# A Fourier mixing layer and a leaky-ReLU feed-forward on one core: folding the sequence rows a second time

## The chip, the cores and the metric

The kernel runs on one core of one Trainium2 chip. The core has a matrix engine (TensorE, PE in the profile; its weight loads are a row of their own, PEld), a vector engine (DVE), a scalar engine (ACT), GpSimd (POOL) and SyncE (SP), which here issues DMAs. Each works through its own list of instructions in order, and waits on semaphores for the others. The metric is the device time of one execution in microseconds; the kernel before takes 2271.5 us (median of 3 runs, 2271.17 to 2273.4).

## What is computed

`x` is [8, 3008, 256] in fp32. Each batch goes through a two-dimensional Fourier transform, over the 3008 sequence rows and over the 256 features, of which the real part is kept. The result, taken as 24064 tokens of 256 features, goes through a feed-forward of width 2048:

```python
X = np.fft.fft(x, axis=1)
X = np.fft.fft(X, axis=2)
x = X.real.astype(np.float32).reshape(B * S, D)
h = x @ w_in                       # [24064, 2048]
g = np.maximum(0.01 * h, h)
out = (g @ w_out).astype(np.float32)
```

## The kernel before

All matmuls are fp32, and each stands in the trace as two matmul records. The feature transform is folded into `w_in` once: `w_in_part` multiplies the cosine and sine tables into it (`wf`, and `wn` for the one feature d = 128 that has no partner). The weights come as 64-bit words; `to_f32` turns one 128x512 piece into fp32 with seven DVE instructions (L218 to L224). There are eight such conversions for `w_in` and eight for `w_out`.

The sequence transform is a matmul with tables. The host lays `x` out so that a sequence row s stands beside its mirror S - s; `load_x` brings a batch into one x buffer as two DMAs of 1536 KB, and `fold_x` adds each row to its mirror (L170), then takes sums and differences of the features d and 256 - d (L172, L173). After that `z` has some 1505 rows that matter, the even and the odd ones apart, in NI = 6 tiles of 128 rows for each parity. A unit (b, c) is a batch and one half c of the frequencies k: 377 or 376 columns. `dft(u, blk)` makes for one unit and one of the two feature blocks (cosine, sine) two accumulated products, over even rows and over odd rows, of six matmuls each (L262). `butterfly` adds and subtracts the two and so gives both k and H + k (H = S/2). `nyquist(c)` does the same for the feature d = 128 of all eight batches, in 12 matmuls for each c.

Then come 32 blocks of 16 steps. A step (j, f) is `up`: two matmuls (L312) into two PSUM tiles, three DVE instructions (L314, L317, L318) that make the tile `g`, and a leaky ReLU on ACT (L319); and `down` (L329): four matmuls that accumulate `g` into four `sum` tiles. `down` trails `up` by `lag = 2` steps. The PSUM tag `up` has four buffers, which `up`, `dft`, `nyquist` and `w_in_part` share; `g` has five.

What stands around that is placed in the step loop at the end of `tile_fnet_leaky_relu`: two `dft` calls for the next unit in each odd block, `load_x(b + 1)` and `fold_x(b + 1)` once per batch. The order on each engine isn't the written one: a scheduler puts instructions forward when it holds their data ready, and the engine then keeps to that list. So the fold of the next batch stands between the DVE instructions of several steps. Before the loop stand the loads, the fold of batch 0, the eight conversions of `w_in`, the first unit's `dft`, and the eight conversions of `w_out`.

Of the kernel before, what the change touches and what calls it, by code (L numbers as in the profile page):

```python
# [28 lines left out]
F32 = mybir.dt.float32  # L32
I32 = mybir.dt.int32
U32 = mybir.dt.uint32
ALU = mybir.AluOpType
ACT = mybir.ActivationFunctionType

B, S, D, F = 8, 3008, 256, 2048
P = 128
H, Q = S // 2, S // 4  # L40
NI = 6
K0 = [0, 377]
KW = [377, 376]
KC = 377
NF = F // P
# [1 line left out]
SLOPE = 0.01  # L47


def m_order():  # L50

    m = np.full((P, NI), -1)
    for i in range(5):
        m[:, i] = 1 + P * i + np.arange(P)
    m[0:112, 5] = 641 + np.arange(112)
    m[112, 5] = 0
    return m


def laid_out(x):  # L60


    m = m_order()
    rows = np.where(m[:, :, None] < 0, S, 2 * m[:, :, None] + np.arange(2))
    mirrors = np.where(rows == S, S, (S - rows) % S)
    d = np.concatenate([np.arange(P + 1), np.arange(D - 1, P, -1)])
    x = np.concatenate([x, np.zeros((B, 1, D), x.dtype)], axis=1)
    return np.stack([x[:, rows][..., d], x[:, mirrors][..., (D - d) % D]], axis=1)


def seq_tables():

    m = m_order()
    out = np.zeros((4, 2, P, NI, KC), np.float32)
    for r in range(2):
        ok = (m >= 0) & ((m < Q) if r == 1 else True)
        weight = np.where(ok, 1.0, 0.0)
        if r == 0:
            weight = np.where((m == 0) | (m == Q), 0.5, weight)
        for c in range(2):  # L80
            k = K0[c] + np.arange(KW[c])
            turn = ((2 * m[:, :, None] + r) * k) % S
            turn = np.where(turn > H, turn - S, turn)
            a = 2.0 * np.pi * turn / S
            cos = np.where(4 * np.abs(turn) == S, 0.0, np.cos(a))
            sin = np.where(np.abs(turn) == H, 0.0, np.sin(a))
            out[r, c, :, :, : KW[c]] = weight[:, :, None] * cos
            out[2 + r, c, :, :, : KW[c]] = weight[:, :, None] * sin
    return out
# [28 lines left out]
def columns():

    at = np.zeros(B * S, np.int64)  # L120
    for b, c, sg, first, n in chunks()[0]:
        k = K0[c] + np.arange(n)
        plus, minus = (k, (S - k) % S) if sg == 0 else ((H + k) % S, H - k)
        at[b * S + minus] = first + n + np.arange(n)
        at[b * S + plus] = first + np.arange(n)
    return at
# [3 lines left out]
def tile_fnet_leaky_relu(  # L130
# [10 lines left out]
    nc = tc.nc  # L141
    PS = bass.MemoryType.PSUM
    const = ctx.enter_context(tc.tile_pool(name="const", bufs=1))
    xp = ctx.enter_context(tc.tile_pool(name="xp", bufs=1))
# [7 lines left out]
    def dft_ps():  # L152
        return up_ps("dft_ps")
# [1 line left out]
    xs = {}  # L155

    def load_x(b):
        t = xp.tile([P, 2, NI, 2, D], F32, tag="x", bufs=1, name="xt")
        for h in range(2):
            nc.sync.dma_start(t[:, h], x[b, h])  # L160
        xs[b] = t

    zs = {}

    def fold_x(b):

        t = xs.pop(b)
        s = t[:, 0].rearrange("p i r d -> p (i r) d")
        z = t[:, 1].rearrange("p i r d -> p (i r) d")
        nc.vector.tensor_tensor(s, s, z, op=ALU.add)  # L170
        lo, hi = s[:, :, 1:P], s[:, :, P + 1 : D]
        nc.vector.tensor_tensor(z[:, :, 1:P], lo, hi, op=ALU.add)  # L172
        nc.vector.tensor_tensor(z[:, :, P + 1 : D], lo, hi, op=ALU.subtract)  # L173
        nc.scalar.copy(z[:, :, 0:1], s[:, :, 0:1])
        nc.gpsimd.memset(z[:, :, P : P + 1], 0.0)
        zs[b] = z


    feat_sb = const.tile([P, 2, 2 * P + 2], F32, name="feat_sb")
    nc.sync.dma_start(feat_sb, feat_tab.rearrange("(a p) n -> p a n", p=P))  # L180
    load_x(0)
    wf = const.tile([P, 2, F], F32, name="wf")
    wn = const.tile([P, NF], F32, name="wn")
    wo = const.tile([P, NF, D], F32, name="wo")
    nyx = const.tile([P, 2, NI, 2, B], F32, name="nyx")
    nya = nyx[:, 0]
    tabs = {}

    def load_tab(q, n, c):
        t = const.tile([P, NI, KC], F32, name=f"tab_{n}_{c}")  # L190
        q.dma_start(t, seq_tab[n, c])
        tabs[n, c] = t
# [54 lines left out]
    def w_out_part(f):  # L247
        nf = WN // D
        raw = load_w(w_out[f * P : (f + nf) * P, :].rearrange("(c p) d -> p c d", p=P))
        to_f32(wo[:, f : f + nf, :].rearrange("p c d -> p (c d)"), raw, w_out.dtype)  # L250

    fold_x(0)
    for n in range(4):
        load_tab(nc.scalar, n, 0)
# [4 lines left out]
    def sequence(ps_t, m, z_of, n, c):  # L259

        for i in range(NI):
            nc.tensor.matmul(ps_t[0:m, 0 : KW[c]], lhsT=z_of(i), rhs=tabs[n, c][:, i, 0 : KW[c]],  # L262
                             start=(i == 0), stop=(i == NI - 1))

    def butterfly(plus, minus, even_ps, odd_ps, m, kw):
        ev = work.tile([P, KC], F32, tag="ev", bufs=2, name="ev")
        nc.scalar.copy(ev[0:m, 0:kw], even_ps[0:m, 0:kw])  # L267
        nc.vector.tensor_tensor(plus, ev[0:m, 0:kw], odd_ps[0:m, 0:kw], op=ALU.add)  # L268
        nc.vector.tensor_tensor(minus, ev[0:m, 0:kw], odd_ps[0:m, 0:kw], op=ALU.subtract)  # L269

    def dft(u, blk):

        b, c = u
        z, kw = zs[b], KW[c]
        t = work.tile([P, 2, KC], F32, tag=f"mix{blk}", bufs=2, name=f"mix{blk}")
        pe, po = dft_ps(), dft_ps()
        for r, pt in ((0, pe), (1, po)):
            sequence(pt, P, lambda i: z[:, 2 * i + r, blk * P : (blk + 1) * P], 2 * blk + r, c)
        butterfly(t[:, 0, 0:kw], t[:, 1, 0:kw], pe, po, P, kw)
        mixed.setdefault(u, {})[blk] = t  # L280


    nc.vector.tensor_tensor(nya, nya, nyx[:, 1], op=ALU.add)
    nyq_dram = dram.tile([B, 2, 2, KC], F32, name="nyq_dram")

    def nyquist(c):
        pe, po = dft_ps(), dft_ps()
        for r, pt in ((0, pe), (1, po)):
            sequence(pt, B, lambda i: nya[:, i, r, :], r, c)
        t = work.tile([P, 2, KC], F32, tag="mix0", bufs=2, name="nyq")  # L290
        butterfly(t[0:B, 0, 0 : KW[c]], t[0:B, 1, 0 : KW[c]], pe, po, B, KW[c])
        nc.sync.dma_start(nyq_dram[:, c, :, 0 : KW[c]], t[0:B, :, 0 : KW[c]])
# [29 lines left out]
    def down(j, f):  # L322
# [8 lines left out]
        if f == NF - 1:  # L331
            for h in range(2):
                o = work.tile([P, 2, KC], F32, tag="o", bufs=2, name="o")
                for i in range(2):
                    nc.scalar.copy(o[:, i, 0:n], sums[j][h][i][:, 0:n])  # L335
                nc.sync.dma_start(out[h * P : (h + 1) * P, first : first + 2 * n].rearrange("p (i n) -> p i n", i=2),
                                  o[:, :, 0:n])

    nyquist(0)
    dft(units[0], 0)  # L340
    dft(units[0], 1)
    spread(units[0])
# [53 lines left out]
```

## Time and profile before

| what | value |
|---|---|
| median of 3 runs | 2271.5 us |
| the profiled execution's own time | 2273.85 us |
| its span, first to last instruction | 2272.1 us |
| PE busy | 2229.8 us, 98% |
| DVE busy | 963.7 us, 42% |
| ACT busy | 502.7 us, 22% |
| DMA, mean rate | 33 GB/s |
| mean granted TensorE clock | 0.998 of full speed |

The busy times are averages over two quite different stretches: a start of some 65 us, in which loads and conversions run, and the loop. The profiled execution lies 1.75 us over its span, and 2.35 us over the median.

### The profile page before, as it was taken

The page shows a single profiled execution, that of the slowest core. Times are in us where ns is not written, and L with a number is a line of the kernel's source. Part 1 is how long each engine was busy: PE and PEld are TensorE (multiplying, and loading weights), DVE is VectorE, ACT ScalarE, POOL GpSimd, SP SyncE. Part 2 cuts the span into 40 slices and gives each one's busy share as a digit, 9 for nine tenths or more (in the row PEclk, how much of TensorE's full clock was granted, in tenths as well). Part 3 has the DMA queues.
Part 4 walks back from the last instruction along what each step waited for, and adds up shares of the span by engine and source line. Part 5 has one row for each costly group of instructions (what it writes and reads, how often), then busy time and mean ns, then how long its engine had stood idle before and what let it go on. Part 6 is the DMA issues. An engine that isn't in the chain of part 4 may idle for free.

```text
span 2272.1 us, 18025 instructions
## 1 busy us (share of the span) xinstructions
PE 2229.8 (98%) x7056; PEld 1329.0 (58%) x7056; DVE 963.7 (42%) x1741; ACT 502.7 (22%) x696; POOL 1.2 (0%) x12
## 2 busy tenths in 40 slices
PE   3999999999999999999999999999999999999999
PEld 1555655555555565555555556555655555555565
DVE  5734434344343433435334353334434344343343
ACT  0122222222122221222222122221222222222222
POOL 0000000000000000000000000000000000000000
PEclk9999999999999999999999999999999999999999
DMA  7201000010000200001000100001000010000000
GB/s 299 89 14 61 16 14 21 14 74 2 14 21 14 76 14 1 21 29 62 14 8 14 70 21 14 21 14 56 21 14 21 14 62 14 14 21 14 14 14 14
DMA packets 23965, 75.23 MB, mean 33 GB/s; under 512 B 1968, under 2 KB 12608, under 8 KB 20808
## 3 DMA queue, kind: packets, MB, share of 16 engines
q1 hardware_dynamic: 22728, 64.82, 7.7%
q10 hardware_dynamic: 1152, 9.27, 1.0%
q8 instruction: 55, 0.90, 0.2%
q14 instruction: 30, 0.25, 0.0%
HBM read 49.35 MB, written 24.72 MB: 33 GB/s over the span
## 4 chain that ended last, share of the span: by engine, by line
PE 98%; DMA 1%; DVE 1%; SPq 0%; issue 0%; ACT 0%; DVEq 0%
PE sum_ps L329 57%; PE cos_ps L312 14%; PE sin_ps L312 14%; PE dft_ps L262 11%; DMA raw<-in_w_in_dram 1%; PE up_ps L238 0%; PE up_ps L243 0%; DVE win L224 0%; DVE raw L223 0%; DVE raw L219 0%; DVE raw L222 0%; DVE xt L172 0%; DVE xt L173 0%; DVE raw L218 0%; DVE raw L221 0%; DVE raw L220 0%
## 5 line engine op out<-in xcount | busy, mean ns | idle before, releaser
L329 PE MATMUL sum_ps<-g,wo 128*128 128x377 f32 (+1 forms) x4096 | 1379.4, 479 | 0.0
L329 PEld LDWEIGHTS sum_ps<-g,wo 128*128 128x128 f32 x4096 | 777.1, 190 | 519.4 <-ACT g L319 0.2
L319 ACT ACTIVATE g<-g 128x752 f32<-128x752 f32 (+1 forms) x512 | 426.0, 832 | 1516.6 <-DVE g L318 1513.6
L314 DVE SCALAR_TENSOR_TENSOR cos<-nb,wn,cos_ps 128x376 f32<-128x376 f32 (+1 forms) x512 | 310.5, 607 | 1007.9 <-PE cos_ps L312 1007.9
L312 PE MATMUL sin_ps<-mix,wf 128*128 128x376 f32 (+1 forms) x1024 | 407.4, 479 | 0.0
L312 PE MATMUL cos_ps<-mix,wf 128*128 128x376 f32 (+1 forms) x1024 | 406.7, 478 | 0.0
L317 DVE TENSOR_TENSOR g<-cos,sin_ps 128x376 f32<-128x376 f32 (+1 forms) x512 | 280.3, 547 | 62.9 <-DVE cos L314 1.9
L318 DVE TENSOR_TENSOR g<-cos,sin_ps 128x376 f32<-128x376 f32 (+1 forms) x512 | 276.8, 541 | 0.0
L312 PEld LDWEIGHTS sin_ps<-mix,wf 128*128 128x128 f32 x1024 | 194.1, 190 | 129.9
L312 PEld LDWEIGHTS cos_ps<-mix,wf 128*128 128x128 f32 x1024 | 193.0, 189 | 130.9 <-issue 0.6
L262 PE MATMUL dft_ps<-tab,xt 128*128 128x377 f32 (+1 forms) x768 | 248.4, 479 | 0.0
L262 PEld LDWEIGHTS dft_ps<-tab,xt 128*128 128x128 f32 x768 | 145.3, 189 | 98.2 <-issue 0.6
L268 DVE TENSOR_TENSOR mix<-ev,dft_ps 128x377 f32<-128x377 f32 (+1 forms) x32 | 17.5, 547 | 196.3 <-PE dft_ps L262 189.8
L335 ACT COPY o<-sum_ps 128x376 f32<-128x376 f32 (+1 forms) x128 | 53.9, 474 | 77.5 <-PE sum_ps L329 77.5
L238 PE MATMUL up_ps<-win,feat_sb 128*128 128x512 f32 x32 | 19.9, 758 | 38.2 <-DVE win L224 38.2
L170 DVE TENSOR_TENSOR xt<-xt 128x3072 f32<-128x3072 f32 x8 | 26.8, 3352 | 22.3 <-DMA xt<-in_x_dram 22.3
L238 PEld LDWEIGHTS up_ps<-win,feat_sb 128*128 128x128 f32 x32 | 6.4, 222 | 45.4 <-DVE win L224 39.1
L267 ACT COPY ev<-dft_ps 128x377 f32<-128x377 f32 (+3 forms) x34 | 16.1, 473 | 75.7 <-PE dft_ps L262 75.7
L269 DVE TENSOR_TENSOR mix<-ev,dft_ps 128x377 f32<-128x377 f32 (+1 forms) x32 | 17.3, 541 | 0.0
L262 PE MATMUL dft_ps<-tab,nyx 128*8 128x377 f32 (+1 forms) x48 | 15.7, 479 | 0.0
L172 DVE TENSOR_TENSOR xt<-xt 128x1524 f32<-128x1524 f32 x8 | 13.9, 1738 | 0.0
L173 DVE TENSOR_TENSOR xt<-xt 128x1524 f32<-128x1524 f32 x8 | 13.9, 1737 | 0.0
(24 smaller groups left out, 94.7 us busy)
## 6 DMA issues: line engine op xcount, KB each, us to landing
xt<-in_x_dram SPq DMA_DIRECT2D x16, 1536.0 KB, 9.5
out_dram<-o SPq DMA_DIRECT2D x32, 377.0 KB, 2.6
out_dram<-o SPq DMA_DIRECT2D x32, 376.0 KB, 2.8
tab<-in_seq_tab_dram ACTq DMA_DIRECT2D x8, 1131.0 KB, 10.0
raw<-in_w_in_dram SPq DMA_DIRECT2D x8, 512.0 KB, 3.9
raw<-in_w_out_dram SPq DMA_DIRECT2D x8, 512.0 KB, 3.7
nb<-nyq_dram SPq DMA_DIRECT2D x8, 377.0 KB, 3.3
nb<-nyq_dram SPq DMA_DIRECT2D x8, 376.0 KB, 4.0
```

The source lines that it names most:

```text
L170: nc.vector.tensor_tensor(s, s, z, op=ALU.add)
L238: nc.tensor.matmul(pt, lhsT=feat_sb[:, a, w * P : (w + 1) * P], rhs=win[a], start=(a == 0), stop=(a == 1))
L262: nc.tensor.matmul(ps_t[0:m, 0 : KW[c]], lhsT=z_of(i), rhs=tabs[n, c][:, i, 0 : KW[c]], start=(i == 0), stop=(i == NI - 1))
L268: nc.vector.tensor_tensor(plus, ev[0:m, 0:kw], odd_ps[0:m, 0:kw], op=ALU.add)
L269: nc.vector.tensor_tensor(minus, ev[0:m, 0:kw], odd_ps[0:m, 0:kw], op=ALU.subtract)
L312: nc.tensor.matmul(pt[blk][:, 0:n], lhsT=wf[:, blk, fs], rhs=mixed[b, c][blk][:, sg, 0:n], start=True, stop=True)
L314: nc.vector.scalar_tensor_tensor(cos[:, 0:n], in0=spreads[b, c][:, sg, 0:n], scalar=wn[:, f : f + 1], in1=pt[0][:, 0:n], op0=ALU.mult, op1 ...
L317: nc.vector.tensor_tensor(g[:, 0, 0:n], cos[:, 0:n], pt[1][:, 0:n], op=ALU.add)
L318: nc.vector.tensor_tensor(g[:, 1, 0:n], cos[:, 0:n], pt[1][:, 0:n], op=ALU.subtract)
L319: nc.scalar.activation(g[:, :, 0:n], g[:, :, 0:n], ACT.Lrelu)
L329: nc.tensor.matmul(sums[j][h][i][:, 0:n], lhsT=wo[:, f, h * P : (h + 1) * P], rhs=g[:, i, 0:n], start=(f == 0), stop=(f == NF - 1))
L335: nc.scalar.copy(o[:, i, 0:n], sums[j][h][i][:, 0:n])
```

## The change

The fold is done twice. The host now lays four rows together, s, S - s, H - s and H + s, for s up to S/4, and `fold_x` first adds the mirrors (one instruction over both halves of the buffer), then takes the feature sums and differences for each half, and then adds and subtracts the two halves. The sum serves the even k, the difference the odd k (for the sine block the other way round, `(c + blk) % 2`). So a unit's c now means the parity of k and no longer the lower or upper half; the column counts stay 377 and 376. Each product over rows has NI = 3 tiles where it had 6, and each table half the bytes. `nyquist` gets the same second fold in two more small instructions. The x buffers become two.

```diff
-NI = 6
-K0 = [0, 377]
+NI = 3
...
-            k = K0[c] + np.arange(KW[c])
-            turn = ((2 * m[:, :, None] + r) * k) % S
+            k = 2 * np.arange(KW[c]) + c
+            turn = (s[:, :, None] * k) % S
...
     def load_x(b):
-        t = xp.tile([P, 2, NI, 2, D], F32, tag="x", bufs=1, name="xt")
+        t = xp.tile([P, 2, 2, NI * 2, D], F32, tag="x", bufs=2, name="xt")
         for h in range(2):
-            nc.sync.dma_start(t[:, h], x[b, h])
+            nc.sync.dma_start(t[:, h], x[b, :, h].rearrange("p e i r d -> p e (i r) d"))
         xs[b] = t
...
     def fold_x(b):
 
+
         t = xs.pop(b)
-        s = t[:, 0].rearrange("p i r d -> p (i r) d")
-        z = t[:, 1].rearrange("p i r d -> p (i r) d")
-        nc.vector.tensor_tensor(s, s, z, op=ALU.add)
-        lo, hi = s[:, :, 1:P], s[:, :, P + 1 : D]
-        nc.vector.tensor_tensor(z[:, :, 1:P], lo, hi, op=ALU.add)
-        nc.vector.tensor_tensor(z[:, :, P + 1 : D], lo, hi, op=ALU.subtract)
-        nc.scalar.copy(z[:, :, 0:1], s[:, :, 0:1])
-        nc.gpsimd.memset(z[:, :, P : P + 1], 0.0)
-        zs[b] = z
+        a, z = t[:, :, 0], t[:, :, 1]
+        nc.vector.tensor_tensor(a, a, z, op=ALU.add)
+        for h in range(2):
+            lo, hi = a[:, h, :, 1:P], a[:, h, :, P + 1 : D]
+            nc.vector.tensor_tensor(z[:, h, :, 1:P], lo, hi, op=ALU.add)
+            nc.vector.tensor_tensor(z[:, h, :, P + 1 : D], lo, hi, op=ALU.subtract)
+            nc.scalar.copy(z[:, h, :, 0:1], a[:, h, :, 0:1])
+            nc.gpsimd.memset(z[:, h, :, P : P + 1], 0.0)
+        nc.vector.tensor_tensor(a[:, 0], z[:, 0], z[:, 1], op=ALU.add)
+        nc.vector.tensor_tensor(a[:, 1], z[:, 0], z[:, 1], op=ALU.subtract)
+        zs[b] = a
...
-            sequence(pt, P, lambda i: z[:, 2 * i + r, blk * P : (blk + 1) * P], 2 * blk + r, c)
+            sequence(pt, P, lambda i: z[:, (c + blk) % 2, 2 * i + r, blk * P : (blk + 1) * P], 2 * blk + r, c)
...
-    nc.vector.tensor_tensor(nya, nya, nyx[:, 1], op=ALU.add)
+    nya, nyb = nyx[:, :, 0], nyx[:, :, 1]
+    nc.vector.tensor_tensor(nyb, nya, nyb, op=ALU.add)
+    nc.vector.tensor_tensor(nya[:, 0], nyb[:, 0], nyb[:, 1], op=ALU.add)
+    nc.vector.tensor_tensor(nya[:, 1], nyb[:, 0], nyb[:, 1], op=ALU.subtract)
```

The change also moves instructions, since the second x buffer lets a load and its fold go forward. In the lists below the changed kernel's lines are 3 to 8 higher than before's: its L223 to L229 are the seven instructions of a conversion, L173 is the first instruction of the fold, L176 and L177 are the feature sums and differences, L180 and L181 the second fold, L322, L325 and L326 the three of `up`.

DVE at the start, the second conversion of `w_in`, before:

```order
L218 TENSOR_SCALAR raw_105<-raw_102 128x512
L220 TENSOR_SCALAR raw_105<-raw_102 128x512
L219 SCALAR_TENSOR_TENSOR raw_105<-raw_102,raw_105 128x512
L221 TENSOR_SCALAR raw_105<-raw_105 128x512
L222 TENSOR_SCALAR raw_105<-raw_105 128x512
L223 SCALAR_TENSOR_TENSOR raw_105<-raw_102,raw_105 128x512
L224 SCALAR_TENSOR_TENSOR win_104<-raw_105 128x512
```

And the same conversion now, where `xt_816` is the second x buffer, batch 1:

```order
L223 TENSOR_SCALAR raw_111<-raw_108 128x512
L225 TENSOR_SCALAR raw_111<-raw_108 128x512
L224 SCALAR_TENSOR_TENSOR raw_111<-raw_108,raw_111 128x512
L226 TENSOR_SCALAR raw_111<-raw_111 128x512
L173 TENSOR_TENSOR xt_816<-xt_816 128x2x1536
L227 TENSOR_SCALAR raw_111<-raw_111 128x512
L176 TENSOR_TENSOR xt_816<-xt_816 128x6x127
L228 SCALAR_TENSOR_TENSOR raw_111<-raw_108,raw_111 128x512
L177 TENSOR_TENSOR xt_816<-xt_816 128x6x127
L229 SCALAR_TENSOR_TENSOR win_110<-raw_111 128x512
```

The fold of batch 1 has moved from the loop into conversions 2 to 4 of `w_in` (its other four instructions stand in conversions 3 and 4). On SP the two loads of batch 1 have moved with it, in front of the second and the third load of `w_in`.

DVE at the end of the start, the last conversion of `w_out` and the first step, before:

```order
L223 SCALAR_TENSOR_TENSOR raw_394<-raw_392,raw_394 128x512
L224 SCALAR_TENSOR_TENSOR wo_76<-raw_394 128x512
L268 TENSOR_TENSOR nyq_416<-ev_417,dft_ps_403 8x376
L269 TENSOR_TENSOR nyq_416<-ev_417,dft_ps_403 8x376
L314 SCALAR_TENSOR_TENSOR cos_426<-nb_312,wn_75,cos_ps_422 128x377
L317 TENSOR_TENSOR g_428<-cos_426,sin_ps_423 128x377
L318 TENSOR_TENSOR g_428<-cos_426,sin_ps_423 128x377
```

And now, from the last row but one of the fifth conversion of `w_out` on:

```order
L325 TENSOR_TENSOR g_412<-cos_410,sin_ps_407 128x377
L229 SCALAR_TENSOR_TENSOR wo_76<-raw_354 128x512
L223 TENSOR_SCALAR raw_364<-raw_362 128x512
L225 TENSOR_SCALAR raw_364<-raw_362 128x512
L224 SCALAR_TENSOR_TENSOR raw_364<-raw_362,raw_364 128x512
L226 TENSOR_SCALAR raw_364<-raw_364 128x512
L326 TENSOR_TENSOR g_412<-cos_410,sin_ps_407 128x377
L227 TENSOR_SCALAR raw_364<-raw_364 128x512
L322 SCALAR_TENSOR_TENSOR cos_420<-nb_302,wn_75,cos_ps_416 128x377
L228 SCALAR_TENSOR_TENSOR raw_364<-raw_362,raw_364 128x512
L325 TENSOR_TENSOR g_422<-cos_420,sin_ps_417 128x377
```

Before, the first step came behind all eight conversions; now the first four steps stand between the instructions of the last four conversions.

DVE in the loop, where a fold stands between steps (before it is batch 1, `xt_844`):

```order
L314 SCALAR_TENSOR_TENSOR cos_855<-nb_312,wn_75,cos_ps_851 128x377
L170 TENSOR_TENSOR xt_844<-xt_844 128x3072
L317 TENSOR_TENSOR g_857<-cos_855,sin_ps_852 128x377
L318 TENSOR_TENSOR g_857<-cos_855,sin_ps_852 128x377
L314 SCALAR_TENSOR_TENSOR cos_869<-nb_312,wn_75,cos_ps_865 128x377
L172 TENSOR_TENSOR xt_844<-xt_844 128x12x127
L317 TENSOR_TENSOR g_871<-cos_869,sin_ps_866 128x377
```

And now, at the same step of the same block (it is batch 2, `xt_1830`):

```order
L322 SCALAR_TENSOR_TENSOR cos_827<-nb_302,wn_75,cos_ps_823 128x377
L173 TENSOR_TENSOR xt_1830<-xt_1830 128x2x1536
L325 TENSOR_TENSOR g_829<-cos_827,sin_ps_824 128x377
L326 TENSOR_TENSOR g_829<-cos_827,sin_ps_824 128x377
L322 SCALAR_TENSOR_TENSOR cos_841<-nb_302,wn_75,cos_ps_837 128x377
L176 TENSOR_TENSOR xt_1830<-xt_1830 128x6x127
L325 TENSOR_TENSOR g_843<-cos_841,sin_ps_838 128x377
L326 TENSOR_TENSOR g_843<-cos_841,sin_ps_838 128x377
L177 TENSOR_TENSOR xt_1830<-xt_1830 128x6x127
L322 SCALAR_TENSOR_TENSOR cos_855<-nb_302,wn_75,cos_ps_851 128x377
```

The fold begins at the same place, three steps behind the `dft` that frees its buffer, a batch further ahead, and goes over four steps: one with L173, two with two feature instructions each, one with L180 and L181.

## Rows read from the trace of the kernel before

**Rows 1.** The page, busy time, share and instructions of each engine.
```profile
PE 2229.8 (98%) x7056; PEld 1329.0 (58%) x7056; DVE 963.7 (42%) x1741; ACT 502.7 (22%) x696; POOL 1.2 (0%) x12
```
**Rows 2.** By stretch: length, busy PE, PEld, DVE, ACT, POOL; clock, DMA share, GB/s.
```profile
100.00:2260.00 2160.00, 2160.00 (x6828) 1293.29 (x6827) 893.30 (x1610) 489.13 (x671) 0.84 (x7) 1.00 0.07 24
```
**Rows 3.** The chain that ended last: start us, us, what.
```profile
66.79 28.92 PE dft_ps L262 x90
...
160.57 7.59 PE dft_ps L262 x24
...
297.24 7.62 PE dft_ps L262 x24
...
2104.88 7.59 PE dft_ps L262 x24
```
**Rows 4.** Timeline of DVE, 22 to 34 us: start us, us, what, idle before.
```profile
22.33 3.36 DVE L170 TENSOR_TENSOR xt<-xt 128x3072 f32<-128x3072 f32 x1 [22.33 <-DMA xt<-in_x_dram]
...
26.64 1.74 DVE L172 TENSOR_TENSOR xt<-xt 128x1524 f32<-128x1524 f32 x1
28.30 1.74 DVE L173 TENSOR_TENSOR xt<-xt 128x1524 f32<-128x1524 f32 x1
...
30.89 0.25 DVE L283 TENSOR_TENSOR nyx<-nyx 128x96 f32<-128x96 f32 x1
```
**Rows 5.** DVE by stretch: length, busy, clock, DMA share, GB/s.
```profile
22.33:96.72 74.39, 65.94 (x124) 0.95 0.50 177
```
**Rows 6.** Timeline of DVE, 58 to 99 us: a wait in a conversion, first steps.
```profile
58.51 0.69 DVE L224 SCALAR_TENSOR_TENSOR win<-raw 128x512 f32<-128x512 f32 x1 [2.39 <-PE up_ps L243]
...
96.72 0.59 DVE L314 SCALAR_TENSOR_TENSOR cos<-nb,wn,cos_ps 128x377 f32<-128x377 f32 x1
...
98.34 0.60 DVE L314 SCALAR_TENSOR_TENSOR cos<-nb,wn,cos_ps 128x377 f32<-128x377 f32 x1
```
**Rows 7.** The chain: the `down` matmuls of the fourth step.
```profile
111.12 2.54 PE sum_ps L329 x8
```
**Rows 8.** Busy time by stretch, 2 to 22 us and 42 to 60 us.
```profile
2.00:22.00 20.00, 0.00 (x0) 0.00 (x0) 0.00 (x0) 0.00 (x0) 0.00 (x0) 1.00 0.98 407
42.00:50.00 8.00, 5.85 (x25) 3.63 (x26) 7.34 (x16) 1.33 (x3) 0.00 (x0) 1.00 0.39 131
50.00:53.00 3.00, 2.46 (x6) 1.05 (x4) 2.83 (x6) 0.00 (x0) 0.00 (x0) 0.61 0.53 175
53.00:57.00 4.00, 3.88 (x7) 1.82 (x7) 2.88 (x7) 0.65 (x2) 0.00 (x0) 0.50 0.42 131
```
**Rows 9.** Timeline of PE, 45 to 57 us.
```profile
45.47 1.98 PE L238 MATMUL up_ps<-win,feat_sb 128*128 128x512 f32 x4 [1.50 <-DVE win L224]
...
53.12 3.78 PE L238 MATMUL up_ps<-win,feat_sb 128*128 128x512 f32 x4 [0.66 <-DVE win L224]
```
**Rows 10.** The page, DMA issues: KB each, median us to landing.
```profile
xt<-in_x_dram SPq DMA_DIRECT2D x16, 1536.0 KB, 9.5
...
tab<-in_seq_tab_dram ACTq DMA_DIRECT2D x8, 1131.0 KB, 10.0
```
**Rows 11.** Timeline of DVE, 201 to 221 us, around a fold in the loop.
```profile
202.96 0.54 DVE L318 TENSOR_TENSOR g<-cos,sin_ps 128x377 f32<-128x377 f32 x1
205.58 0.61 DVE L314 SCALAR_TENSOR_TENSOR cos<-nb,wn,cos_ps 128x377 f32<-128x377 f32 x1 [2.08 <-PE cos_ps L312]
...
209.91 3.35 DVE L170 TENSOR_TENSOR xt<-xt 128x3072 f32<-128x3072 f32 x1
...
220.80 0.61 DVE L314 SCALAR_TENSOR_TENSOR cos<-nb,wn,cos_ps 128x377 f32<-128x377 f32 x1 [0.45 <-PE cos_ps L312]
```
**Rows 12.** Timeline of PE, the second `up` after that step's.
```profile
208.55 0.80 PE L312 MATMUL cos_ps<-mix,wf 128*128 128x377 f32 x2
```
**Rows 13.** Timeline of SP: the loads of batch 1 go out.
```profile
198.64 0.82 SPq L160 DMA_DIRECT2D xt<-in_x_dram  x2
```
**Rows 14.** The load line's instructions, time from issue to landing.
```profile
DMA to landing us min/median/max: 6.1/9.5/20.5
```

More of the change, by code (lines that the diff above doesn't have):

```diff
@@ L47, with m_order, taken @@
 SLOPE = 0.01
[L50 to L57, printed above, removed]
+def m_order(r):
+    m = np.arange(P)[:, None] + P * np.arange(NI)
+    return np.where(m < (377, 376)[r], m, -1)
 def laid_out(x):
-    m = m_order()
-    rows = np.where(m[:, :, None] < 0, S, 2 * m[:, :, None] + np.arange(2))
-    mirrors = np.where(rows == S, S, (S - rows) % S)
+    m = np.stack([m_order(0), m_order(1)], axis=-1)
+    rows = 2 * m + np.arange(2)
     d = np.concatenate([np.arange(P + 1), np.arange(D - 1, P, -1)])
     x = np.concatenate([x, np.zeros((B, 1, D), x.dtype)], axis=1)
-    return np.stack([x[:, rows][..., d], x[:, mirrors][..., (D - d) % D]], axis=1)
+    def taken(rows, d):
+        return x[:, np.where(m < 0, S, rows % S)][..., d]
+    mirrored = (D - d) % D
+    return np.stack([
+        np.stack([taken(rows, d), taken(S - rows, mirrored)], axis=2),
+        np.stack([taken(H - rows, d), taken(H + rows, mirrored)], axis=2),
+    ], axis=2)
 def seq_tables():
-    m = m_order()
     out = np.zeros((4, 2, P, NI, KC), np.float32)
     for r in range(2):
[L76 to L79, printed above, removed]
+        m = m_order(r)
+        s = 2 * m + r
+        weight = np.where(m < 0, 0.0, np.where((s == 0) | (s == Q), 0.5, 1.0))
         for c in range(2):
-            k = K0[c] + np.arange(KW[c])
-            turn = ((2 * m[:, :, None] + r) * k) % S
+            k = 2 * np.arange(KW[c]) + c
+            turn = (s[:, :, None] * k) % S
             turn = np.where(turn > H, turn - S, turn)
@@ L121, in columns @@
     for b, c, sg, first, n in chunks()[0]:
-        k = K0[c] + np.arange(n)
+        k = 2 * np.arange(n) + c
         plus, minus = (k, (S - k) % S) if sg == 0 else ((H + k) % S, H - k)
@@ L184, in tile_fnet_leaky_relu @@
     wo = const.tile([P, NF, D], F32, name="wo")
-    nyx = const.tile([P, 2, NI, 2, B], F32, name="nyx")
-    nya = nyx[:, 0]
+    nyx = const.tile([P, 2, 2, NI, 2, B], F32, name="nyx")
     tabs = {}
@@ L288, in nyquist @@
         for r, pt in ((0, pe), (1, po)):
-            sequence(pt, B, lambda i: nya[:, i, r, :], r, c)
+            sequence(pt, B, lambda i: nya[:, c, i, r, :], r, c)
         t = work.tile([P, 2, KC], F32, tag="mix0", bufs=2, name="nyq")
@@ L374 @@
         "x": x,
-        "x_nyq": x[..., P].transpose(2, 1, 3, 4, 0),
+        "x_nyq": x[..., P].transpose(1, 2, 3, 4, 5, 0),
         "w_in": moe_w_in,
```

## The prediction

> **What bounds the kernel now.** I read the busy times first: PE is busy for 2229.8 of 2272.1 us, DVE for 963.7 [rows 1]. A share over the whole span hides stages, so I looked by stretch: between 100 and 2260 us PE is busy for 2160.00 of 2160.00 us, at the full clock [rows 2]. Nothing else can be the bound there, and a matmul taken out shortens the time by its own length, as long as no other engine falls behind. The reader is to see that "busy" is the right number in this case: the chain of waits runs through PE's records without a gap, and gives the lengths end to end. A piece of 24 records of the sequence transform takes 7.59 us with 376 columns and 7.62 us with 377 [rows 3], so 0.316 us a record, two records to a matmul.
>
> The start is another kernel. DVE waits until x lands at 22.33 us [rows 4], DMA being the bound until then (407 GB/s, engines 98% busy [rows 8]). From there to 96.72 us, where the first step begins, DVE is busy for 65.94 of 74.39 us [rows 5], while PE takes its parts of `w_in` whenever a conversion is done, and from 66.79 us on has 28.92 us of transforms [rows 3]. So DVE and PE end the start nearly together: at 95.71 us PE is through, at 96.72 DVE.
>
> **PE in the loop.** Units 1 to 15 have two `dft` pieces each, 30 pieces of 24 records, of which the first, one with 377 columns and the last are shown [rows 3]; 16 belong to units with 376 columns and 14 to units with 377. Each piece keeps 12 records. What goes is 16 x 3.795 + 14 x 3.81 = 60.7 + 53.3 = 114.1 us. The `up` and `down` matmuls stay as they are, and so do the column counts. PE waits for nothing there, so all of it should come off the span, if DVE keeps pace.
>
> **DVE in the loop.** The old fold has 3072, 1524 and 1524 elements: 3.36 us and twice 1.74, of which a follower hides 0.08 (L172 and L173 start 1.66 apart) [rows 4]. The lengths give (3.36 - 1.74) / 1548 = 1.05 ns an element. By that an instruction of 762 elements takes some 0.87 us start to start and one of 1536 some 1.67. The new fold is 3.28 + 4 x 0.87 + 2 x 1.67 = 10.1 us where the old one was 6.6. It is off PE's path if DVE's delay stays below what the loop allows. A step is 12 records on PE, 3.8 us, in which DVE idles 2.08 [rows 11]. The three instructions of the step that ends at 202.96 + 0.54 = 203.5 us free the PSUM tiles that the second next `up` takes at 208.55 [rows 11, 12]: 5.05 us to spare. The worst delay now is after L173: 3.28 - 2.08 = 1.2 us; two steps with 1.74 us each take 0.7 back, the step with the two halves of 3.34 brings 1.3, so at most some 1.8. The old fold did the same, 3.35 us in one step [rows 11], and DVE was back at waiting for PE by 220.80 us without a gap on PE. So I cost the six folds of the loop at nothing; uncovered they would be 6 x 10.1 = 61 us. The two ACT copies and the two memsets of a fold stand far in front of L180, which waits for them.
>
> The second buffer leaves the place of a load as it was: issued at 198.64 us, when the transform that reads the buffer is through [rows 13], its fold begins at 209.91 [rows 11]. 11.3 us stand against landings of 9.5 us in the middle [rows 14]. It carries the same bytes, in 12 KB for each partition as before, so I add no wait.
>
> **The start.** Here the gain isn't to be had. PE's 90 records become 42, 28.92 x 42 / 90 = 13.5 us, 15.4 less. But DVE gets more: the first fold's 3.5 us, 0.35 us for two more small instructions like L283, and now also the whole fold of batch 1, 10.1 us, in conversions 2 to 4: 13.9 us. And the eight conversions of `w_out`, which ran beside 28.92 us of transforms, now run beside 13.5, and the first four steps wait between their instructions. So I follow DVE to the end of the fourth step. A step costs it 98.34 - 96.72 = 1.62 us [rows 6], four cost 6.5. Without any idle: 22.33 + 65.94 + 13.9 + 6.5 = 108.7 us. Before, 74.39 - 65.94 = 8.45 us of idle lay in it [rows 5]; kept whole that is 117.1, and two more waits for a slow PE of 2.39 us [rows 6] make 121.9. The ReLU and the handing over add 0.9, so the fourth `down` would begin between 109.6 and 122.8, where before it began at 111.12 [rows 7]: 1.5 us earlier to 11.7 later.
>
> x can land earlier, since the tables are half as big. Up to 22 us, 20 x 0.407 = 8.1 MB came in, of which x and the feature table are 3.4, the tables some 4.7 [rows 8, 10]. In the changed kernel all eight tables are 4.6 MB; if six are in front of x it lands 1.2 MB, 3 us, earlier, if all are, no earlier. SP now has batch 1's two loads in front of the second and third of `w_in`: 3.1 MB. With x, feature table, all tables and three pieces of `w_in` that makes 12.7 MB, in by some 33 us at 0.407 MB/us; DVE has the first fold, until 30 us or later, and two conversions to do before it comes to the third, so I expect no wait there. The bounds are -4.5 and +11.7 us. Of the idle I keep 6 us: the fold of batch 1 fills the waits for `w_in`, the waits for PE stay and grow. That gives 114.7 + 0.9, 4.5 later; some 0.5 for PE at the lower clock in the first transforms; 2 off for x. I take +3 us, at the middle of the bounds.
>
> Here the clock bears on the price. PE ran the `w_in` parts at the full clock first, 1.98 us for a group of four records; with PE busy 5.85 of 8 us the clock then fell to 0.61 and 0.50 of full speed (1.2 GHz), and the same group took 3.78 us [rows 8, 9]. The fold of batch 1 draws these groups apart. If they all run at the lower level, the waits are those of 2.39 us that stand in the upper bound; if at the higher, they are gone.
>
> The Trainium skill's page "TensorE: Matmul & The Clock Gate", section "Why this matters for your kernels", says to avoid idle gaps between matmul bursts, since they put the clock back to half. The trace agrees, with 0.50 at 53 to 57 us after gaps of 1.5 us. It speaks against this change at the start, where the gaps get longer; the third rival is what it would do there, 2170 us where I say 2161.
>
> **The sum.** 2272.1 - 114.1 + 3 = 2161.0 us of span; 1.75 outside it and 2.35 from the profiled execution to the median: 2160.4. I say 2161 us, 0.951 of the time before.
>
> **Rivals.**
> *The start keeps its gain.* The fold of batch 1 fits into DVE's 8.45 us of idle, and the conversions hide beside the first steps; then 15.4 us go as well, 2161 - 3 - 15 = 2143 us. For it: PE has the slack to run ahead. Against it: DVE alone needs until 108.7 us.
> *The folds hold up the loop.* If a fold's delay passes the 5.05 us by as much again, six cost up to 30 us: 2161 + 15 to 30 = 2176 to 2191 us. For it: 10.1 us in four steps whose idle is 8.3. Against it: it is spread, and the old fold's L170 alone, of 3.35 us, left no mark.
> *The lower clock in the whole start.* The groups of `w_in` and the first transforms at 1.2 GHz, PE waiting between the first four steps: the upper bound, 2161 + 9 = 2170 us, a little more if the 13.5 us of transforms double in part.
> *Slower than before: a fold waits for its load, and DVE stands.* L173 stands in DVE's list before the instructions of several steps; if the load of the batch after next lands late, they wait behind it, then PE's `up` for PSUM, while the load itself had to wait for PE's transform. The price is a landing's excess over 11.3 + 5 us, six times. Slower begins at (114.1 - 3) / 6 = 18.5 us of standing, a landing of 35 us. That would come if the load left one piece later, six steps of 3.8 us and a piece of 3.8, 26.6 us: 26.6 + 9.5 - 16.3 = 19.8 us each, 119 in all, 2280 us. Against it: the list has the load where it was, and no fold of the loop waited.
>
> **How the numbers follow.** The forecast has 0.75, the gain at the start 0.06, held-up loop 0.06, low clock 0.11, slower 0.02. From the bounds of the start the forecast's own times go from 2153 to 2169; the range takes in the low clock and one or two microseconds a fold, and a little of the gain at the start: 2150 to 2175. What this measurement can tell from no change is some 0.2%, 4.5 us; every case but the last lies far on the faster side: faster 0.97, same 0.01, slower 0.02.
>
> **What would show it.** Right: the chain has 30 pieces of 12 records at 3.8 us, PE is busy without a gap from some 125 us on, and the fourth `down` begins at 110 to 120 us, behind DVE, not behind PE. Wrong in the loop: PE waits for DVE's L326 or for the ReLU in the four steps around each L173, or L173 waits for a DMA. Wrong at the start: the first step's L322 is reached before the conversions end without a wait on PE, or batch 1 lands after DVE comes to its fold, which would delay all conversions behind it. The forecast as a whole is wrong if the loop's PE time doesn't fall by 114 us.

## The result, and the profile after

The changed kernel takes 2158.72 us (median of 4 runs, 2156.96 to 2159.75) against 2272.45 us of the kernel before on the same chip: a ratio of 0.9499, interval [0.9483, 0.9516]. The profiled execution took 2157.95 us with a span of 2155.8. The forecast was a span of 2161.0 and a time of 2161 us. The loop did what was forecast; the start came out 2.2 us shorter where I had put 3 us longer. By "start" I mean all that comes before the fourth `down`: 111 us in the kernel before, of which the 65 us named with its profile are only the part up to the last of `w_in`. The time missed the forecast by 2.3 us and the span by 5.2: this profiled execution lies 0.8 us under the median, the one before lay 2.35 over it, and that the time came out nearer than the span is luck.

The page's busy line, for [rows 1], and the stretch behind the start, for [rows 2] (length, busy PE, PEld, DVE, ACT, POOL; clock, DMA share, GB/s):

```profile
PE 2106.6 (98%) x6648; PEld 1256.3 (58%) x6648; DVE 988.6 (46%) x1775; ACT 499.9 (23%) x704; POOL 1.7 (0%) x20
```
```profile
100.00:2145.00 2045.00, 2045.00 (x6463) 1224.22 (x6462) 911.82 (x1641) 485.33 (x676) 0.85 (x12) 1.00 0.07 24
```

7056 - 6648 = 408 matmul records are gone: 30 x 12 of the loop and 48 of the start. PE is again busy without a gap, so the loop is shorter by the records that went. The chain (start, us, what), for [rows 3, 7]:

```profile
2.85 17.52 DMA tab<-in_seq_tab_dram
20.38 12.90 DMA xt<-in_x_dram
33.37 3.36 DVE xt L173
...
108.88 2.54 PE sum_ps L337 x8
...
158.34 3.79 PE dft_ps L267 x12
...
287.42 3.81 PE dft_ps L267 x12
```

The pieces have 12 records and 3.79 and 3.81 us, as forecast. The fourth `down` begins at 108.88 us, 2.24 earlier than in [rows 7]; 2272.1 - 114.1 - 2.2 = 2155.8 us, which is the span. So two numbers hold the whole result, and only the second needs explaining. The chain already names a suspect: from 20.38 to 36.7 us it runs through the load and the fold of batch 1, which the kernel needs only some 200 us later.

DVE at the start, its timeline (start, us, what, idle before), for [rows 4]:

```profile
16.47 3.36 DVE L173 TENSOR_TENSOR xt<-xt 128x3072 f32<-128x3072 f32 x1 [16.47 <-DMA xt<-in_x_dram]
...
20.94 0.95 DVE L177 TENSOR_TENSOR xt<-xt 128x762 f32<-128x762 f32 x1
21.80 0.95 DVE L176 TENSOR_TENSOR xt<-xt 128x762 f32<-128x762 f32 x1
...
24.13 1.75 DVE L180 TENSOR_TENSOR xt<-xt 128x1536 f32<-128x1536 f32 x1
25.80 1.75 DVE L181 TENSOR_TENSOR xt<-xt 128x1536 f32<-128x1536 f32 x1
...
33.37 3.36 DVE L173 TENSOR_TENSOR xt<-xt 128x3072 f32<-128x3072 f32 x1 [1.45 <-DMA xt<-in_x_dram]
```

x landed at 16.47 us, 5.86 earlier than in [rows 4]. The new instructions cost what the line through the old ones gave: 0.86 start to start (0.87 forecast) and 1.67 (1.67). Batch 1's fold waited 1.45 us for its load. DVE's balance to the end of the fourth step, for [rows 5], and the DMA before x lands, for [rows 8]:

```profile
16.47:106.87 90.40, 83.35 (x150) 0.92 0.47 164
```
```profile
2.00:16.00 14.00, 0.00 (x0) 0.00 (x0) 0.00 (x0) 0.18 (x1) 0.00 (x0) 1.00 0.97 388
```

DVE is busy 83.35 of 90.40 us. The loop's first fold on DVE, for [rows 11]:

```profile
199.56 0.61 DVE L322 SCALAR_TENSOR_TENSOR cos<-nb,wn,cos_ps 128x377 f32<-128x377 f32 x1 [2.09 <-PE cos_ps L320]
200.09 3.35 DVE L173 TENSOR_TENSOR xt<-xt 128x3072 f32<-128x3072 f32 x1
...
210.97 0.61 DVE L322 SCALAR_TENSOR_TENSOR cos<-nb,wn,cos_ps 128x377 f32<-128x377 f32 x1 [0.31 <-PE cos_ps L320]
...
218.58 0.61 DVE L322 SCALAR_TENSOR_TENSOR cos<-nb,wn,cos_ps 128x376 f32<-128x376 f32 x1 [1.12 <-PE cos_ps L320]
```

DVE is back at waiting for PE after three steps and again after the last, and PE shows no wait.

### The profile page after: what moved, and what is told of

Its sections match the earlier page's. It is cut to its first block, busy times and chain, and to the rows that moved or that the text cites. A ratio compares the mean times of both kernels' runs of the same rounds, so it can differ in the third digit from the quotient of the medians.

```text
span 2155.8 us, 17264 instructions
## 1 busy us (share of the span) xinstructions
PE 2106.6 (98%) x6648; PEld 1256.3 (58%) x6648; DVE 988.6 (46%) x1775; ACT 499.9 (23%) x704; POOL 1.7 (0%) x20
## 4 chain that ended last, share of the span: by engine, by line
PE 97%; DVE 1%; DMA 1%; issue 0%; ACTq 0%; ACT 0%; DVEq 0%
PE sum_ps L337 60%; PE sin_ps L320 15%; PE cos_ps L320 15%; PE dft_ps L267 6%; DMA tab<-in_seq_tab_dram 1%; PE up_ps L243 1%; DMA xt<-in_x_dram 1%; PE up_ps L248 0%; DVE win L229 0%; DVE raw L224 0%; DVE xt L173 0%; DVE raw L228 0%; DVE raw L227 0%; DVE raw L226 0%; DVE raw L225 0%
## 5 line engine op out<-in xcount | busy, mean ns | idle before, releaser
L322 DVE SCALAR_TENSOR_TENSOR cos<-nb,wn,cos_ps 128x376 f32<-128x376 f32 (+1 forms) x512 | 310.6, 607 | 988.6 <-PE cos_ps L320 988.6
L325 DVE TENSOR_TENSOR g<-cos,sin_ps 128x376 f32<-128x376 f32 (+1 forms) x512 | 280.4, 548 | 61.9 <-DVE cos L322 1.9
L326 DVE TENSOR_TENSOR g<-cos,sin_ps 128x376 f32<-128x376 f32 (+1 forms) x512 | 277.1, 541 | 0.0
L267 PE MATMUL dft_ps<-tab,xt 128*128 128x377 f32 (+1 forms) x384 | 126.8, 479 | 0.0
L267 PEld LDWEIGHTS dft_ps<-tab,xt 128*128 128x128 f32 x384 | 72.7, 190 | 49.2 <-issue 0.6
L173 DVE TENSOR_TENSOR xt<-xt 128x3072 f32<-128x3072 f32 x8 | 26.8, 3355 | 17.9 <-DMA xt<-in_x_dram 17.9
L177 DVE TENSOR_TENSOR xt<-xt 128x762 f32<-128x762 f32 x16 | 15.2, 949 | 0.0
L176 DVE TENSOR_TENSOR xt<-xt 128x762 f32<-128x762 f32 x16 | 15.2, 948 | 0.0
## 6 DMA issues: line engine op xcount, KB each, us to landing
tab<-in_seq_tab_dram ACTq DMA_DIRECT2D x8, 565.5 KB, 14.0
```

The costliest lines, as they stand in the source:

```text
L173: nc.vector.tensor_tensor(a, a, z, op=ALU.add)
L322: nc.vector.scalar_tensor_tensor(cos[:, 0:n], in0=spreads[b, c][:, sg, 0:n], scalar=wn[:, f : f + 1], in1=pt[0][:, 0:n], op0=ALU.mult, op1 ...
L325: nc.vector.tensor_tensor(g[:, 0, 0:n], cos[:, 0:n], pt[1][:, 0:n], op=ALU.add)
L326: nc.vector.tensor_tensor(g[:, 1, 0:n], cos[:, 0:n], pt[1][:, 0:n], op=ALU.subtract)
```

## The experiments

Six runs take the start apart, four test the loop. Ratios are against the kernel before in the same job; differences in us are between medians of different jobs, in which the kernel before took 2271.25 to 2272.47 us. Spans are those of the profiled executions.

**One x buffer: what the fold of batch 1 costs at the start.**

```diff
-        t = xp.tile([P, 2, 2, NI * 2, D], F32, tag="x", bufs=2, name="xt")
+        t = xp.tile([P, 2, 2, NI * 2, D], F32, tag="x", bufs=1, name="xt")
```

> The changed kernel with one x buffer, so that the fold of batch 1 goes back into the loop. Theory (the start is bound by DVE's list): 10.1 us of fold and the wait of 1.45 us for batch 1's load leave the start, the fourth down begins at some 98 us instead of 108.88, the time falls from 2158.7 to 2148.5 us, give or take 2. Rival (the second buffer is needed in the loop, or PE bounds the start): the loop has waits at its folds and the time stays or rises, 2158 to 2170.

Measured: 2147.18 us (0.9449 [0.9437, 0.9462]), 11.5 less. The chain of this kernel:

```profile
1.71 13.99 DMA xt<-in_x_dram
15.79 3.36 DVE xt L173
...
98.07 2.54 PE sum_ps L337 x8
```

The fourth `down` begins 10.8 us earlier, the span is 2145.0 = 2155.8 - 10.8. The fold cost DVE 10.1 us and its wait 1.45, and x lands 0.7 us earlier without batch 1's load: 12.2 us, of which 10.8 came back. The conversions between which the fold stood are busy 0.8 us longer without it (54.1 us for 53.3, summed over the timelines), and the other waits and the handing over to PE grew by 0.6. In the loop the same fold stands between steps and costs nothing.

**Tables behind x on the same queue: what the tables cost x.** The tables go out on SP's queue behind x and the first weights instead of on ACT's beside them.

```diff
-    for n in range(4):
-        load_tab(nc.scalar, n, 0)
     for f0 in range(0, F, WN):
         w_in_part(f0)
+        if f0 == 0:
+            for n in range(4):
+                load_tab(nc.sync, n, 0)
...
-        load_tab(nc.scalar, n, 1)
+        load_tab(nc.sync, n, 1)
```

> The changed kernel with the table loads put behind x on SP's queue. Theory (DVE begins when x lands, and everything behind it moves along): x lands at some 10.5 us instead of 16.47, the fourth down begins 6 us earlier, 2152.7 us, give or take 2. Rival (the waits behind x, for w_in, batch 1 and PE, take it up): 2157 to 2159.

Measured: 2154.61 us (0.9483 [0.947, 0.9496]), 4.1 less. x landed at 11.48 us, 5.0 earlier, and the span fell by 4.5: what x gains at the head of the chain is kept nearly whole. The edit moves more than the tables: batch 1's load goes out later, and its fold begins behind four conversions, at 42.79 us instead of 33.37.

**Both together.**

> Both: one x buffer and the tables behind x. If both act on the same DVE list they add: 2158.7 - 10.2 - 6 = 2142.5 us. If PE or the loads of w_in become the bound of the start, less than that: 2146 to 2150.

Measured: 2142.40 us (0.9429 [0.9416, 0.9442]). 11.5 and 4.1 would give 2143.1: the two add, so they are different terms of one sum.

**One buffer, tables padded to their old bytes.** Each table is loaded with as many zeros behind it; nothing reads them.

```diff
-        t = const.tile([P, NI, KC], F32, name=f"tab_{n}_{c}")
+        t = const.tile([P, 2 * NI, KC], F32, name=f"tab_{n}_{c}")
...
-        "seq_tab": seq_tables(),
+        "seq_tab": np.concatenate([seq_tables(), np.zeros((4, 2, P, NI, KC), np.float32)], axis=3),
```

> One x buffer, and the tables padded with zeros to the bytes they had before, 1131 KB each; the added half is loaded and not used. It undoes the halving of the table bytes alone. Theory: x lands at 22.3 us again, 5.9 later, and the time is 5.9 us over that with one x buffer. Rival (idle in DVE's list absorbs it): 0 to 2 us over.

Measured: 2152.20 us (0.9472 [0.9459, 0.9485]), 5.0 more than with one buffer; x landed at 20.78 us, 4.99 later. The table's bytes move x, and x moves the end, us for us.

**The transforms doubled again: is the loop's gain the records alone?**

```diff
-        for i in range(NI):
+        tiles = list(range(NI)) * times
+        for at, i in enumerate(tiles):
...
+                     times=1 if u == units[0] else 2)
```

> The changed kernel, but every unit after the first accumulates its 3 row tiles twice, so each of its 30 transform pieces has 24 records again (its part of the transform comes out doubled; folds, tables, buffers and the start stay as they are). Theory: the loop's gain is nothing but the 12 records taken out of each piece; 16 x 3.795 + 14 x 3.81 = 114.1 us come back, 2158.7 + 114.1 = 2272.8 us, pieces of 7.59 and 7.62 us in the chain, PE without a gap. Rival (part of the loop's gain comes from the new fold or the second buffer, or the longer fold costs something that the shorter loop hides): the time differs from 2272.8 by more than 3 us.

Measured: 2273.77 us (1.0006 [0.9997, 1.0016]), 115.1 more than the changed kernel; its pieces take 7.59 and 7.62 us and PE doesn't wait. The theory holds: halved tiles are the loop's whole gain. The rest of the change, with the start as it is, is worth nothing that this measurement can tell from zero.

**Five times the second fold in small pieces, and lumps: how much cover DVE has.** In the first, batches 2 to 7 repeat the second fold's two instructions. In the other two (with one x buffer) one long instruction stands at the end of each fold; the second cut below is the longer one, and the shorter has 3 where it has 6:

```diff
-        nc.vector.tensor_tensor(a[:, 0], z[:, 0], z[:, 1], op=ALU.add)
-        nc.vector.tensor_tensor(a[:, 1], z[:, 0], z[:, 1], op=ALU.subtract)
+        for _ in range(1 if b < 2 else 5):
+            nc.vector.tensor_tensor(a[:, 0], z[:, 0], z[:, 1], op=ALU.add)
+            nc.vector.tensor_tensor(a[:, 1], z[:, 0], z[:, 1], op=ALU.subtract)
```
```diff
+        if b > 0:
+            blob = work.tile([P, 6, NI * 2, D], F32, tag="blob", bufs=1, name="blob")
+            many = a[:, 0].unsqueeze(1).broadcast_to([P, 6, NI * 2, D])
+            nc.vector.tensor_tensor(blob, many, many, op=ALU.add)
```

> The changed kernel with the second fold's two instructions (1.75 us each) done five times instead of once for batches 2 to 7: 8 more instructions, 13.4 us of DVE for each of six folds, 80 us in all, in small pieces. Theory (the fold of the loop is covered by DVE's 2.08 us of idle a step): within 2 us of the changed kernel, 2158.7, DVE busy some 80 us more, PE without a gap in the loop. Rival (the fold is on the path): up to 80 us more, 2239 us.

> The same with lumps of 4608 elements, 4.8 us. Theory: DVE is late by 4.8 - 2.1 = 2.7 us, with what is left of the fold's own delay some 3.7, below 5.05: no change, 2147 +- 2 us, no gap on PE. Rival (the slack is smaller than I read from the rows): 1 to 4 us seven times, 2154 to 2175 us.

> The kernel with one x buffer (2147.2 us, spans 2145.0), plus one DVE instruction of 9216 elements at the end of each of the seven folds in the loop, in one piece: at 1.05 ns an element 9.7 us, into a tile that nothing reads. Theory (DVE may fall behind by the 5.05 us until PE wants the PSUM tiles again, and by little more): behind a lump DVE is late by 9.7 - 2.1 idle = 7.6 us, of which 5.05 are covered, so PE stands 2 to 4 us seven times, 2161 to 2175 us. Rival 1 (all of it hidden, DVE's average alone counts): 2147. Rival 2 (DVE's work adds in full): 2147 + 68 = 2215 us.

Measured: 2159.30 us for the five-fold fold (0.9498 [0.9482, 0.9514]; 0.6 more, DVE busy 1062.3 us, 74 more), 2147.45 with lumps of 4.95 us (0.9449 [0.9435, 0.9463]; 0.3 more), both without a wait of PE behind the start; but 2198.17 with lumps of 9.75 us (0.9673 [0.9658, 0.9687]), 51.0 more. That is neither the 14 to 28 that I expected nor the 68 of rival 2. The waits of PE, then DVE and PE around the first lump (of that kernel's lines L326 and L330 are the first and last of a step, L324 is `up`, L341 `down`), and a stretch of PE behind it:

```profile
PE sin_ps L324 <- DVE g L330: 32.5, 7, 4.6
```
```profile
180.51 0.61 DVE L326 SCALAR_TENSOR_TENSOR cos<-nb,wn,cos_ps 128x377 f32<-128x377 f32 x1 [2.10 <-PE cos_ps L324]
...
181.69 0.54 DVE L330 TENSOR_TENSOR g<-cos,sin_ps 128x377 f32<-128x377 f32 x1
...
199.53 0.61 DVE L326 SCALAR_TENSOR_TENSOR cos<-nb,wn,cos_ps 128x377 f32<-128x377 f32 x1 [0.31 <-PE cos_ps L324]
...
204.31 0.60 DVE L326 SCALAR_TENSOR_TENSOR cos<-nb,wn,cos_ps 128x377 f32<-128x377 f32 x1
204.82 9.75 DVE L186 TENSOR_TENSOR blob<-xt 128x9216 f32<-128x9216 f32 x1
...
214.95 0.54 DVE L330 TENSOR_TENSOR g<-cos,sin_ps 128x377 f32<-128x377 f32 x1
```
```profile
210.11 0.79 PE L324 MATMUL cos_ps<-mix,wf 128*128 128x376 f32 x2
215.54 1.62 PE L324 MATMUL sin_ps<-mix,wf 128*128 128x376 f32 x2 [4.64 <-DVE g L330]
216.96 4.13 PE L341 MATMUL sum_ps<-g,wo 128*128 128x377 f32 x8
220.93 0.79 PE L324 MATMUL cos_ps<-mix,wf 128*128 128x376 f32 x2
```
```profile
215.00:221.00 6.00, 5.46 (x11) 3.11 (x12) 3.34 (x8) 3.81 (x6) 0.00 (x0) 0.60 0.00 0
```

The step of the lump should have begun one step, 3.80 us, behind 199.53, at 203.33, and ended 181.69 + 0.54 - 180.51 = 1.72 later, at 205.05. It ended at 215.49, 10.4 us late: the idle of 2.08 us that I took off stands behind L330 and not between L326 and L329, where the lump is, and 1 us of delay came from the fold. PE stands from 215.54 - 4.64 = 210.90; so the cover is 210.90 - 205.05 = 5.85 us, near the 5.05 that I read from the rows. The lump of 4.95 us is 9.75 - 4.95 = 4.8 us less late, 5.6, and PE shows no wait: the cover lies where the rows have it, and beyond it, at the one size tried, every us is PE's.

Seven waits are 32.5 us. The other 18.5 are the clock: behind the first wait `sin` and the `down` take 220.93 - 215.54 = 5.39 us for ten records, where 3.16 is usual, with a granted clock of 0.60 on the average of 215 to 221 us and single records at twice their time, the lower level (1.2 GHz). That is 2.2 us more at this fold. The same ten records take 4.67 to 6.32 us behind the seven waits, 18.1 us more than usual in all, with a granted clock of 0.50 to 0.72 in the 6 us of each. I had priced a wait by its length alone.

**Six of the eight conversions of `w_out` inside the first block: is it DVE that ends the start?**

```diff
-    for f in range(0, NF, WN // D):
+    for f in (0, 2):
...
+            if j == 0 and f % 2 == 0 and f + 4 < NF:
+                w_out_part(f + 4)
```

> The changed kernel, but only two of the eight pieces of w_out are converted before the loop; the other six are converted in the first block, each one step or more ahead of the down that reads it. Theory (DVE bounds the start: between the last conversion of w_in and the fourth step it has the conversions of w_out to do, and PE, with 15.4 us less of transforms, waits for it): the first steps come as soon as PE's transforms are through; the fourth down begins near 102 us instead of 108.88, the conversions go into the 2.08 us of idle of each step, and the time is some 7 us less, 2151.7 us. Rival (PE, its clock or the nyquist round trip holds the first steps anyway, or the six conversions of 5 us come back as gaps of PE in the first block): 2158 us or more.

Measured: 2150.99 us (0.9466 [0.9453, 0.9479]), 7.7 less. The chain of that kernel:

```profile
101.99 2.54 PE sum_ps L337 x8
```

The fourth `down` begins at 101.99, where 102 was expected, 6.9 us earlier than in the changed kernel, and the span is 2148.9, 6.9 less; PE doesn't wait in the block that now holds the six conversions. So PE's 15.4 us were partly to be had, once DVE was unloaded.

**All three together.**

> One x buffer, the tables on SP's queue behind x, and six pieces of w_out converted in the first block, all three together. Theory (the parts act on different stretches of the start: batch 1's fold, the landing of x, the conversions of w_out): 2142.4 - 7 = 2135.4 us. Rival (with the fold of batch 1 gone and x early, PE's own work of w_in parts and transforms ends the start, and the conversions no longer matter): 2140 to 2143 us.

Measured: 2135.43 us (0.9399 [0.9385, 0.9413]), 23.3 us less than the changed kernel. Its fourth `down`:

```profile
87.17 2.54 PE sum_ps L338 x8
```

108.88 - 87.17 = 21.7 us, which is the difference of the spans, 2155.8 - 2134.1. It is the best version that was run: the change, with the start freed of what it needn't do there.

## Why the prediction was right, and where it was off

**The loop, -114.1 us: right.** Records, their times and PE without a gap came as forecast, and doubling the tiles again gave 115.1 back.

**The folds of the loop at nothing: right, and for the reason given.** 74 us more of DVE in small pieces cost 0.6 us; the lumps put the cover at 5.85 us, a little above the 5.05 that I read. The rival that folds hold up the loop needed a delay twice the cover: such a delay does cost, and more than I priced, since the clock falls behind the wait.

**The slower rival, a fold that waits in the loop for its load: not seen.** The waits for x are two, both at the start.

**The start, +3 us: the term that was mis-sized; it was -2.2.** The forecast put the fourth `down` at 111.1 + 3 = 114.1 us, as 20.3 (x) + 86.3 (DVE's work) + 6.5 (idle and lower clock) + 0.9 (handing over). Measured: 16.47 + 83.35 + 7.05 + 2.01 = 108.88. By terms:

- *x landed 5.86 us earlier, not 2 (bound 3): -3.9.* The step that failed is "if six are in front of x it lands 1.2 MB, 3 us, earlier, if all are, no earlier". It counted whole tables. What decides is the tables' share of the DMAs while x comes in. The queues until x landed (packets, MB, share), before and after; q10 is ACT's, with the tables, q1 is SP's, with x:

```profile
q10 hardware_dynamic: 603, 4.88, 54.7%
q1 hardware_dynamic: 592, 3.54, 38.1%
```
```profile
q1 hardware_dynamic: 607, 3.60, 53.2%
q10 hardware_dynamic: 507, 2.08, 36.1%
```

  Of the bytes the tables had 58% and now have 37%, 1.4 and 0.6 bytes for one of SP's queue: a table's row is half as long (1131 and 565.5 KB over 128 partitions), and the two queues still moved about as many packets. Tables padded to their old rows brought x 5.0 us later, tables behind x 5.0 earlier, so the tables are what moved x. The Trainium skill's page "DMA: Bandwidth & Descriptors", section "Queues, rings and completion order", has it that a DMA engine takes turns between the queues packet by packet. The packet counts agree with that; no run here changes a packet's size without a row's.
- *DVE's work 83.35 us, not 86.3: -3.0.* The instructions are those forecast; they overlap better. Before, a conversion by itself takes 3.53 us from its first row to the next one's, and a step 1.62 [rows 6]. Rows of one before:

```profile
67.53 0.43 DVE L218 TENSOR_SCALAR raw<-raw 128x512 int32<-128x512 int32 x1 [0.96 <-DMA raw<-in_w_out_dram]
...
68.81 0.42 DVE L221 TENSOR_SCALAR raw<-raw 128x512 int32<-128x512 int32 x1
69.26 0.43 DVE L222 TENSOR_SCALAR raw<-raw 128x512 int32<-128x512 int32 x1
...
71.06 0.42 DVE L218 TENSOR_SCALAR raw<-raw 128x512 int32<-128x512 int32 x1
```

  Now conversions and steps stand between each other:

```profile
101.76 0.41 DVE L223 TENSOR_SCALAR raw<-raw 128x512 int32<-128x512 int32 x1
...
103.03 0.41 DVE L226 TENSOR_SCALAR raw<-raw 128x512 int32<-128x512 int32 x1
103.37 0.53 DVE L326 TENSOR_TENSOR g<-cos,sin_ps 128x377 f32<-128x377 f32 x1
103.82 0.41 DVE L227 TENSOR_SCALAR raw<-raw 128x512 int32<-128x512 int32 x1
104.16 0.59 DVE L322 SCALAR_TENSOR_TENSOR cos<-nb,wn,cos_ps 128x377 f32<-128x377 f32 x1
104.68 0.67 DVE L228 SCALAR_TENSOR_TENSOR raw<-raw 128x512 int32<-128x512 int32 x1
105.28 0.53 DVE L325 TENSOR_TENSOR g<-cos,sin_ps 128x377 f32<-128x377 f32 x1
105.73 0.67 DVE L229 SCALAR_TENSOR_TENSOR wo<-raw 128x512 f32<-128x512 f32 x1
106.33 0.53 DVE L326 TENSOR_TENSOR g<-cos,sin_ps 128x377 f32<-128x377 f32 x1
```

  From 101.76 to 106.33 a whole conversion and three instructions of steps take 4.57 us; the three take 0.45 + 0.52 + 0.45 start to start, so the conversion took 3.15. Summed over the timelines, the conversions are busy 53.3 us for 55.4 before; the four steps come to 5.7 for the 6.5 that I put, in which gaps were counted as work; folds and small ones lie 0.3 under the forecast. The run with one buffer took a part of the order back (54.1 us); none took the order of the steps alone back.
- *Idle 7.05 us, not 6.5: +0.5.* I expected no wait for batch 1's load, and there were 1.45 us. It landed at 33.3 us, as I had put it, but I asked when the third piece of `w_in` would be there, and batch 1's fold stands earlier, in the second conversion; DVE, early with x, came to it at 31.92. Waits for PE's parts of `w_in` came to 2.7 us, for its transforms to 0.9.
- *Handing over 2.0 us, not 0.9: +1.1.* DVE ends the fourth step at 106.87 us and the ReLU at 107.73, but PE comes to that `down` only at 108.88. The chain leaves DVE already at the first step's L326, which ends at 94.75. PE at that place:

```profile
94.80 1.62 PE L320 MATMUL sin_ps<-mix,wf 128*128 128x377 f32 x2 [2.82 <-DVE g L326]
96.21 3.42 PE L337 MATMUL sum_ps<-g,wo 128*128 128x377 f32 x8
99.47 0.80 PE L320 MATMUL cos_ps<-mix,wf 128*128 128x377 f32 x2
```

  PE waited 2.82 us for that L326, and from 94.80 us on the profile shows it without a gap. So the sign "at 110 to 120 us, behind DVE, not behind PE" did not come: DVE holds up the first steps, and the fourth `down` comes at PE's own pace. Ten records behind that wait took 99.47 - 94.80 = 4.67 us where 3.16 is usual, at a lower clock (see the last rival below). My sum followed DVE to its fourth step and had no term for this; no run shows what the start would take without that wait.

The sum of these is -5.2, the whole miss of the span (2161.0 to 2155.8).

**The rival "the start keeps its gain" (2143 us).** It gave the fold of batch 1 to DVE's idle, and that is wrong: taking the fold out gave 11.5 us. What I set against it, that "DVE alone needs until 108.7 us", came to 16.47 + 83.35 = 99.8 us, still behind the 96 that the rival needs. DVE's load was the reason: with the fold, six conversions and the tables moved away the start lost what the rival promised, and more.

**The rival of the lower clock (2170 us).** The clock was low in part, as these stretches show (same columns as above):

```profile
40.00:70.00 30.00, 25.19 (x79) 13.79 (x80) 26.09 (x49) 4.42 (x10) 0.00 (x0) 0.83 0.35 106
70.00:80.00 10.00, 10.00 (x40) 5.69 (x39) 8.54 (x18) 1.85 (x5) 0.00 (x0) 1.00 0.40 115
95.00:100.00 5.00, 5.00 (x12) 2.87 (x13) 5.00 (x12) 1.26 (x2) 0.00 (x0) 0.73 0.71 244
```

Between 40 and 70 us a mean of 0.83 mixes the two levels; the transforms from 70 us on ran at the full one; behind PE's wait of 2.82 us, in the first steps, it fell once more, to a mean of 0.73. So a part of this rival did come, PE waiting and slow between the first steps: it cost PE 1.5 us in those ten records. It didn't make the start as long as the rival has it: DVE's waits for PE's parts of `w_in` stayed at 2.7 us, little over the 2.6 of before, so the upper bound's two further waits never came. The rule that gaps between bursts of matmuls bring the lower clock (the Trainium skill, "TensorE: Matmul & The Clock Gate", "Why this matters for your kernels") is borne out in its direction by the long lumps, 0.60 behind a wait of 4.64 us, and by these first steps.

## What to carry to other kernels

Where one engine is busy without a gap, take the gain from its records, and look for the error of the forecast in the start: write the start as a chain (landing, work of the bounding engine, idle, handing over) and check each term, and at each handing over which engine waits for which: here PE's last wait for DVE in the start came at the first step, not at the fourth. A second buffer lets a scheduler pull work forward into the stretch where its engine is the bound; here that cost 11.5 us of a gain that the loop would have kept for nothing. Loads that a first step doesn't need belong behind the load that it does, on the same queue.

## What the runs showed of the hardware

- A wait of TensorE cost more than itself: seven waits, 32.5 us in all, made the kernel 51.0 us longer; the ten records behind each took 4.67 to 6.32 us for 3.16, at a mean clock of 0.50 to 0.72.
- An instruction on VectorE that needs the one just before it started later than an independent one (in rows of a conversion, 0.45 us behind a 0.42 us instruction, L222 behind L221, against 0.34, L322 behind L227), so two interleaved sequences were shorter than the same ones in turn: 3.15 for 3.53 us a conversion.
- Two DMA queues moved packets in about equal number, whatever these carried: 603 and 592 with the old tables, 507 and 607 with rows half as long. So the shorter rows took 0.6 bytes for each of x's queue where they had taken 1.4.
